# Last column group of the first batch: filter rows in a slot of their own, loads and results on other queues

## The chip, the cores and the metric

One core of a Trainium2 chip runs the whole program. The metric is the device time of one execution in microseconds (us), lower is better. Five engines work side by side: PE (TensorE, matrix products), ACT (ScalarE), DVE (VectorE), POOL (GpSimd) and SP (SyncE, which here only issues transfers). Each takes its instructions strictly in the order in which they were written. A transfer (DMA) is issued by SP, ACT or POOL, moves in the background, and signals when it has landed.

## The reference

```
X = rfft(x, axis=1)                 # x: 8 batches x 3008 x 256
y = irfft(X * (filt_r + 1j*filt_i)) # a filter for each frequency and column
h = y.reshape(24064, 256) @ w_in    # 256 x 2048
out = (h - tanh(h)) @ w_out         # 2048 x 256
```

The weights come as 64-bit floats and are taken apart into 32-bit values on the chip.

## The kernel before, in words

The transform of 3008 points is split as 64 x 47: a product over 64 points, a turn through DRAM, a product over 47 (folded to 24), the filter, and the same way back. All of batch 0 is transformed first, in a prologue of some 79 us, because nothing else can start without it; then the main loop (from L1341) goes over units of the two large products, with the transforms of the later batches laid between them by hand. The order of every engine's instructions is the order of the code (`tc.manual_schedule()`, L1006): nothing is moved by a scheduler, so a waiting instruction holds up all that stands behind it on its engine.

In the prologue the 32 column positions are handled in seven groups: g0 to g5 have five positions (120 rows of a tile), the last one, g6, has two (48 rows). Since 48 rows would fill less than half of the partitions, g6 folds its 256 columns: the second 128 columns go to rows 48 to 95 (`extent`, L154; `KL` = 48, `KH` = 96). For each group:

- `across` (L1057) transposes the first product into a tile `a2` of rows; for g6 it then calls `under` (L1076), which copies the second half of the columns to the lower rows by a transfer on SP.
- `forth` (L403) multiplies by the 24 x 24 matrices; DVE makes sums and differences (L421, L422).
- `filters_of` (L1079) loads the filter rows of the group into one of three slots `filt[g % 3]`: on POOL for g0 and g1, on SP from g2. So g6 takes the slot of g3 and can be loaded only after g3 has been filtered. For g6 there are, besides, a small memset on POOL (L1083), rows that were put into reverse order through the DRAM tensor `filt_d` (L1084), eight loads (L1087; the 23 rows of the mirrored frequencies in two loads of 16 and 7), and an `under` for the filters (L1234, run as L1077).
- `filtered` (L425) does the complex product on DVE, with one addition on POOL for g1 to g4 (L442).
- `back0` (L1098), and `back` (L457) for g6, multiply back; ACT copies the result, and a transfer takes it to DRAM (`ct2`): on POOL for g0 to g4, on ACT for g5, and for g6 half on ACT, half on SP (L469).
- `rest` (L1090) reads `ct2` back in the order that the next product needs: four loads for g0 to g4 on POOL, four for g5 and g6 on SP. The first product that needs them is L582, the beginning of the main part.

The loop at L1225 interleaves the groups: in round g it makes `across(g+2)`, loads the filters of g+2, runs `forth` of g+1, filters g, and multiplies g-1 back. In round 2 it also loads the first 8 rows of batch 1, `x1` (`load_x`, L257, three transfers on SP). Between them DVE turns raw weights into 32-bit values (`converted`, L170, called through `weights`, L241); raw weights are loaded on POOL's queue.

After the loop, `first1` (L1187) makes the first product of `x1`: four steps, stored by two transfers of ACT and two of SP; `warmer` keeps PE at work until `ct2` has come back. In the main loop, `filters_d` (L1291) copies the filters into `filt_d` on POOL, two steps at a time (L1411).

Of the kernel before, what the change touches and what calls it, by code (L numbers as in the profile page):

```python
# [32 lines left out]
KL = SLOTS[-1][1] * NH  # L33
KH = 2 * KL
PAD = 32
# [18 lines left out]
def _consts():  # L54
# [35 lines left out]
    for k, (a, b) in enumerate(((cos, cos), (cos, -sin), (sin, cos), (-sin, -sin),  # L90
                                (cos, twice * cos), (cos, -2 * sin),
                                (sin, twice * cos), (-sin, -2 * sin))):
        for row in (0, KL):
# [23 lines left out]
def kernel(  # L117
# [27 lines left out]
    def dram(t, off, dims):  # L145
        return bass.AP(tensor=t, offset=off, ap=[list(d) for d in dims])
# [7 lines left out]
    def extent(g):  # L154

        n = SLOTS[g][1] * NH
        return (n, DM) if g < len(SLOTS) - 1 else (2 * n, DM // 2)

# [202 lines left out]
    def parts(t, b, g, first_block=0, n=4, step=1):  # L361

        a, s = SLOTS[g]
        rows, w = s * NH, extent(g)[1]
        for h in range(DM // w):
            yield (slice(rows * h, rows * (h + 1)), w,
                   dram(t[b], (first_block * NA + a) * NH * DM + w * h,
                        [[DM, rows], [step * NA * NH * DM, n], [1, w]]))
# [637 lines left out]
    with tc.tile_pool(name="tr", bufs=2) as tr, tc.manual_schedule():  # L1006
# [16 lines left out]
        with tc.tile_pool(name="pro", bufs=1) as pro, \  # L1023
                tc.tile_pool(name="ps0", bufs=6, space=bass.MemoryType.PSUM) as ps0:

            def z0(name, shape):
                return ps0.tile(shape, F32, tag="z", bufs=6, name=name)

# [28 lines left out]
            def across(g):  # L1057

                a, s = SLOTS[g]
                n = s * NH  # L1060
                t = buffer("a2")
                for v in (1, 0):
                    pq = z0("pq", [128, 2, DM])
                    for k in range(2):
                        at = (2 * v + k) * NA + a
                        for h in range(2):
                            nc.tensor.transpose(
                                pq[0:n, k, h * 128:h * 128 + 128],
                                turnt[:, h, at:at + s].rearrange("p a r -> p (a r)"), one)
                    copy = ACT.copy if g or v else V.tensor_copy  # L1070
                    copy(t[0:n, 2 * v:2 * v + 2], pq[0:n])
                if g == len(SLOTS) - 1:
                    under(t)
                return t

            def under(t):  # L1076
                nc.sync.dma_start(t[KL:KH, :, 0:DM // 2], t[0:KL, :, DM // 2:DM])  # L1077

            def filters_of(g):  # L1079

                t, queue = filt[g % 3], G if g < 2 else nc.sync
                if g == len(SLOTS) - 1:
                    G.memset(t[0:1, 2:4], 0.0)  # L1083
                    queue.dma_start(t[NH:KL, 2:4], dram(filt_d, (turned * 8 + 5) * DM,  # L1084
                                                        [[8 * DM, NH], [2 * DM, 2], [1, DM]]))
                for v, row, n, src in filter_rows(g):
                    queue.dma_start(t[row:row + n, v], src)  # L1087
                return t
# [9 lines left out]
            def back0(g, nn):  # L1098

                way = ways(g, 1, KM)  # L1100
                for v in range(2):
                    pe = z0("pe", [128, 2, DM])[0:KM]
                    for k in range(2):
# [5 lines left out]
                    ACT.copy(e1, pe)  # L1109
                    (G if g < len(SLOTS) - 2 else ACT).dma_start(  # L1110
                        next(parts(ct2, 0, g, v, 2, 2))[2], e1)

            pairs = []

# [60 lines left out]
            next(turning)  # L1175

            early = weights(tiles0, jobs[:5], G, began, 5)
# [9 lines left out]
            def first1(x1):  # L1187

                for r in range(0, 8, 2):
                    pf = z0("pf", [128, 2, DM])  # L1190
                    for k in range(2):
                        nc.tensor.matmul(pf[:, k], f0[:, r + k], x1[:, r + k],
                                         start=True, stop=True)
# [5 lines left out]
                    (ACT if r < 4 else nc.sync).dma_start(  # L1199
                        dram(ct1[1], r * DM, [[NH * DM, 128], [1, 2 * DM]]), a1)  # L1200
# [3 lines left out]
            convert(5)  # L1204
            last_g = len(SLOTS) - 1
            summed = (last_g,)
# [18 lines left out]
            for g in range(last_g + 1):  # L1225
                if g == 2:
                    x1 = load_x(big([128, 8, DM], F32, "x1"), 1, 0, 8)
                if g + 2 <= last_g:
                    a2[g + 2] = across(g + 2)
                    fts[g + 2] = filters_of(g + 2)  # L1230
                if g == 3:
                    e2s[0] = load_e2(0, 0, ())
                if g == last_g - 1:
                    under(fts[last_g])  # L1234
                if g < last_g:
                    there[g + 1] = there0(g + 1)
                if g == last_g - 1:
                    way_back()
                next(there[g][0])
# [23 lines left out]
            convert(100)  # L1263
            late = weights(tiles1, jobs[5:], G, ahead, 3,
                           after={6: (0,), 8: (1,), 10: (2, 4)})
            next(late)
            for _ in first1(x1):
                pass
            warmer(8)

        with tc.tile_pool(name="dn", bufs=2) as dn, \
# [69 lines left out]
            for U in range(total + 2):  # L1341
# [45 lines left out]
                def t(k):  # L1387
# [80 lines left out]
```

## Time and profile before

| what | us |
|---|---|
| median of 3 runs | 2559.25 (2557.61 to 2559.39) |
| the profiled execution, its own time | 2556.2 |
| span of its trace | 2554.4 |
| PE busy in the span | 2535.7 |
| first product of the main part (L582) with all its data | 79.00 |

The profiled execution took 1.8 us more than its span, which lies before the first and behind the last instruction, and stands 3.05 us under the median. In the rows below, times are microseconds from the start of the span. A row of a timeline gives start, duration, engine, line, operation, output and input, and in brackets the idle time of the engine before it and what ended it; a row of the chain of waits gives start, duration, and the work. SPq, ACTq and POOLq are the issuing of transfers by these engines; the time to the landing of a transfer stands only in the chain.

### The profile page before, as it was taken

Reading aid. Unit: us, or ns where it says so; the run is one execution under the profiler, and the core shown is the slowest. Engines: PE = TensorE matmul, PEld = TensorE weight load, DVE = VectorE, ACT = ScalarE, POOL = GpSimd, SP = SyncE. Lnnn points to the kernel's source line nnn. Section 1 sums busy time; section 2 is a strip of 40 time slices with the busy share of each in tenths; the row PEclk is TensorE's granted clock in tenths of the full one; section 3 lists DMA queues with packets and bytes.
Section 4 is the critical chain, followed back from the end, with each engine's and each line's share of the span. In section 5 each row is a group of like instructions: output and inputs, shape, how many; then the busy total and the mean of one; then the engine's idle time right before and its main releaser. Section 6 shows DMA issues by size and latency. Waiting matters only on the chain.

```text
span 2554.4 us, 44623 instructions
## 1 busy us (share of the span) xinstructions
PE 2535.7 (99%) x17072; PEld 2173.1 (85%) x17072; DVE 1875.8 (73%) x2262; ACT 1667.1 (65%) x2498; POOL 1484.3 (58%) x1129
## 2 busy tenths in 40 slices
PE   9999999999999999999999999999999999999998
PEld 8678889888898888988888888888889888898887
DVE  6887776887678876888668886688866777555555
ACT  4666666666666666666666666666666666666665
POOL 5356665666466665666555665566645666555552
PEclk9999999999999999999999999999999999999999
DMA  8963224322343323342233322443123322110110
GB/s 233 287 163 103 65 53 109 102 65 61 83 102 91 81 64 94 80 111 59 72 95 99 85 63 61 108 100 97 36 67 85 94 66 52 26 32 18 25 22 19
DMA packets 333828, 212.43 MB, mean 83 GB/s; under 512 B 231841, under 2 KB 304959, under 8 KB 329957
## 3 DMA queue, kind: packets, MB, share of 16 engines
q1 hardware_dynamic: 318471, 184.18, 29.3%
q0 software_dynamic: 11616, 17.44, 2.5%
q10 hardware_dynamic: 3518, 7.87, 0.9%
q8 instruction: 136, 2.23, 0.4%
q14 instruction: 87, 0.71, 0.1%
HBM read 128.75 MB, written 83.39 MB: 83 GB/s over the span
## 4 chain that ended last, share of the span: by engine, by line
PE 94%; DMA 3%; DVE 1%; ACT 1%; issue 0%; SPq 0%; POOL 0%; ACTq 0%; POOLq 0%; DVEq 0%
PE o L795 44%; PE x L623 25%; PE z L623 12%; PE y L623 6%; PE pm L401 3%; PE pu L582 2%; DMA x<-in_x_dram 1%; PE pm L340 1%; DMA filt<-in_filt_r_dram 1%; DMA ct<-a 0%; PE o L857 0%; PE pf L297 0%; DMA filt<-filt 0%; DMA ct<-e 0%; DVE wd L231 0%
## 5 line engine op out<-in xcount | busy, mean ns | idle before, releaser
L795 PE MATMUL o<-t,wd 128*128 128x256 f32 (+1 forms) x3008 | 763.4, 376 | 0.0
L603 POOL TENSOR_TENSOR t<-h 128x512 f32<-128x512 f32 (+1 forms) x186 | 305.4, 1642 | 712.7 <-DVE h L745 704.3
L745 DVE TENSOR_TENSOR h<-h,y 128x1024 f32<-128x1024 f32 (+1 forms) x384 | 580.2, 1511 | 160.1 <-ACT y L741 156.6
L795 PEld LDWEIGHTS o<-t,wd 128*128 128x128 f32 x3008 | 568.8, 190 | 85.8 <-POOL o L827 15.1
L623 PE MATMUL x<-tu,wu 128*128 128x256 f32 (+1 forms) x2256 | 576.1, 378 | 0.0
L795 PE MATMUL o<-h,wd 128*128 128x256 f32 (+1 forms) x2256 | 573.4, 377 | 0.2 <-DVE h L745 0.2
L795 PEld LDWEIGHTS o<-h,wd 128*128 128x128 f32 x2256 | 425.6, 190 | 71.3 <-issue 18.4
L629 ACT COPY s<-x 128x512 f32<-128x512 f32 (+1 forms) x188 | 108.6, 578 | 565.0 <-PE x L623 564.5
L623 PEld LDWEIGHTS x<-tu,wu 128*128 128x128 f32 x2256 | 423.3, 190 | 56.9 <-issue 3.9
L738 ACT ACTIVATE y<-y 128x1024 f32<-128x1024 f32 (+1 forms) x384 | 399.4, 1040 | 12.1
L741 ACT ACTIVATE y<-y 128x1024 f32<-128x1024 f32 (+1 forms) x384 | 399.9, 1041 | 4.6
L735 ACT ACTIVATE y<-h 128x1024 f32<-128x1024 f32 (+1 forms) x384 | 400.4, 1043 | 2.5 <-DVE h L671 1.7
L604 POOL TENSOR_TENSOR t<-h,t 128x512 f32<-128x512 f32 (+1 forms) x186 | 313.9, 1688 | 14.6
L606 POOL TENSOR_TENSOR t<-h,t 128x512 f32<-128x512 f32 (+1 forms) x186 | 303.8, 1633 | 0.0
L605 POOL TENSOR_TENSOR t<-h 128x512 f32<-128x512 f32 (+1 forms) x186 | 289.8, 1558 | 0.0
L629 ACT COPY u<-x 128x512 f32<-128x512 f32 (+1 forms) x376 | 213.3, 567 | 57.0 <-PE x L623 54.1
L671 DVE COPY h<-x 128x512 f32<-128x512 f32 (+1 forms) x188 | 127.8, 680 | 127.2 <-PE x L623 127.1
L623 PE MATMUL y<-ut,wu 128*128 128x256 f32 (+1 forms) x752 | 190.2, 375 | 0.7 <-ACT a L299 0.7
L623 PE MATMUL z<-tu,wu 128*128 128x256 f32 (+1 forms) x752 | 190.2, 375 | 0.4 <-DVE h L679 0.4
L623 PE MATMUL z<-ut,wu 128*128 128x256 f32 (+1 forms) x752 | 190.2, 375 | 0.4 <-DVE h L663 0.4
L623 PE MATMUL x<-ut,wu 128*128 128x256 f32 (+1 forms) x752 | 190.1, 375 | 0.0
L663 DVE TENSOR_TENSOR h<-z,u 128x512 f32<-128x512 f32 (+1 forms) x188 | 127.3, 677 | 72.0 <-ACT u L629 71.1
(208 smaller groups left out, 2809.1 us busy)
## 6 DMA issues: line engine op xcount, KB each, us to landing
ft<-filt SPq DMA_DIRECT2D x28, 1024.0 KB
ct<-nn SPq DMA_DIRECT2D x56, 512.0 KB
e<-ct SPq DMA_DIRECT2D x47, 512.0 KB
a<-ct SPq DMA_DIRECT2D x112, 192.0 KB
out_dram<-ot SPq DMA_DIRECT2D x1248, 16.0 KB
x_sb<-in_x_dram SPq DMA_DIRECT2D x110, 128.0 KB
ct<-a SPq DMA_DIRECT2D x60, 128.0 KB
ct<-x_sb SPq DMA_DIRECT2D x60, 128.0 KB
```

The source lines that it names most:

```text
L603: by.tensor_sub(t[0], b[0][1], b[0][0])
L604: by.tensor_sub(t[1], b[1][1], t[0])
L605: by.tensor_sub(t[2], b[1][1], b[0][1])
L606: by.tensor_sub(t[3], b[1][0], t[1])
L623: nc.tensor.matmul(bank[:, k], wu[:, q - 1, (2 * u + k) * 128:(2 * u + k + 1) * 128], rhs[q - 1], start=(first and k == 0), stop=True, ski ...
L629: ACT.copy(t, X)
L671: V.tensor_copy(h[:, 2, :, 0:w], X)
L735: ACT.activation(y[k], ht[k], AF.Arctan, scale=TURN)
L738: ACT.activation(y[k], y[k], AF.Tanh, scale=BEND)
L741: ACT.activation(y[k], y[k], AF.Square, scale=SCALE, accum_out=y_sums[:, 2 * U + k // 2:2 * U + k // 2 + 1])
L745: V.tensor_mul(ht[k], ht[k], y[k])
L795: nc.tensor.matmul(product(q), wd[:, q - 1, (2 * u + k) * 128: (2 * u + k + 1) * 128], rhs[q - 1][:, k], start=(u == 0 and k == 0 and q == ...
```

## The change

- g6 has its second half at partition 64 instead of 48 (`HB`; `KH` becomes 112). `across` brings it there by the transposes themselves: the one for the second half takes 112 columns, the last 48 of which are the wanted ones, and the one for the first half then overwrites the upper 48 rows. The transfer of `under` for `a2` is gone.
- The filter rows of g6 go to a slot of their own, the buffer of the first raw weights (`raw`, three buffers). `filters_of(last_g)` is called in round 2, ahead of `x1`: a memset of 64 x 1024 elements on POOL, then six loads on SP (the 23 mirrored rows in one load). `under` copies them below in round 3 (two transfers on SP), `turned_in` loads the reversed rows in round 4 (two transfers on SP). Before, all of this came in rounds 4 and 5.
- Results of g3 and g4 are stored on SP instead of POOL. `rest` for g0 to g4 is issued on SP instead of POOL, ahead of the last group's results.
- Raw weights 7 and 8 are loaded in round 5 instead of after the loop (so `weights` starts with four begun), and the first step of weight 3 on ACT is called in round 5.
- `first1` stores all four steps on SP, and its first two steps use half of the buffer `xy` instead of `e1`.
- The prologue has 8 PSUM buffers instead of 6. In the main loop the copies of `filters_d` begin one unit later.

```diff
-KH = 2 * KL
+HB = 64
+KH = HB + KL
@@ weights
-                if (after or k > 1) and n == 2 and k + 1 < len(jobs):
+                if (after or k > 2) and n == 2 and k + 1 < len(jobs):
@@ filter_rows, last group
-                for m, n in ((1, 16), (17, 7)):
-                    yield 2 + v, m, n, dram(src, (NQ * m - a - 1) * DM, [[NQ * DM, n], [1, DM]])
+                yield 2 + v, 1, NH - 1, dram(src, (NQ - a - 1) * DM, [[NQ * DM, NH - 1], [1, DM]])
@@ across
-                        for h in range(2):
+                        for h in (0, 1) if w == DM else (1, 0):
+                            lead, col = (0, h * 128) if w == DM else (HB * h, 0)
                             nc.tensor.transpose(
-                                pq[0:n, k, h * 128:h * 128 + 128],
-                                turnt[:, h, at:at + s].rearrange("p a r -> p (a r)"), one)
+                                pq[0:lead + rows, k, col:col + 128],
+                                turnt[:, h].rearrange("p a r -> p (a r)")[:, NH * at - lead:NH * at + rows], one)
-                if g == len(SLOTS) - 1:
-                    under(t)
+            def turned_in(t):
+                for h in range(2):
+                    nc.sync.dma_start(t[HB * h + NH:HB * h + KL, 2:4, 0:DM // 2],
+                                      dram(filt_d, (turned * 8 + 5) * DM + DM // 2 * h,
+                                           [[8 * DM, NH], [2 * DM, 2], [1, DM // 2]]))
             def under(t):
-                nc.sync.dma_start(t[KL:KH, :, 0:DM // 2], t[0:KL, :, DM // 2:DM])
+                for row, end, n in ((0, NH, 4), (NH, KL, 2)):
+                    nc.sync.dma_start(t[HB + row:HB + end, 0:n, 0:DM // 2],
+                                      t[row:end, 0:n, DM // 2:DM])
@@ filters_of
-                if g == len(SLOTS) - 1:
-                    G.memset(t[0:1, 2:4], 0.0)
-                    queue.dma_start(t[NH:KL, 2:4], dram(filt_d, ...))
+                if g == last_g:
+                    t = pro.tile([128, 512], I64, tag="raw", bufs=3, name="filt_end")
+                    t = t.bitcast(F32).rearrange("p (v n) -> p v n", v=4)
+                    G.memset(t[0:HB], 0.0)
@@ back0
-                    (G if g < len(SLOTS) - 2 else ACT).dma_start(
+                    (G if g < 3 else nc.sync if g < last_g - 1 else ACT).dma_start(
@@ first1
-                    if r == 4:
-                        two = tr.tile([128, 2, 2, DM], F32, tag="a1", bufs=1, name="a1")
-                    a1 = (pro.tile([128, 2, DM], F32, tag="e1", bufs=4, name="a1") if r < 4 else
-                          two[:, r // 2 - 2])
+                    if r % 4 == 0:
+                        two = (tr.tile([128, 2, 2, DM], F32, tag="a1", bufs=1, name="a1") if r else
+                               buffer("xy").rearrange("p (m n) c -> p m n c", m=2))
+                    a1 = two[:, r // 2 % 2]
                     ACT.copy(a1, pf)
-                    (ACT if r < 4 else nc.sync).dma_start(
+                    nc.sync.dma_start(
@@ the loop over the groups
                 if g == 2:
+                    fts[last_g] = filters_of(last_g)
                     x1 = load_x(big([128, 8, DM], F32, "x1"), 1, 0, 8)
                 if g + 2 <= last_g:
                     a2[g + 2] = across(g + 2)
-                    fts[g + 2] = filters_of(g + 2)
+                    if g + 2 < last_g:
+                        fts[g + 2] = filters_of(g + 2)
+                    else:
+                        turned_in(fts[last_g])
                 if g == 3:
+                    under(fts[last_g])
                     e2s[0] = load_e2(0, 0, ())
-                if g == last_g - 1:
-                    under(fts[last_g])
                 if g == last_g - 1:
+                    ahead += [begun(tiles1, job, queue=G) for job in jobs[7:9]]
+                    next(began[3])
                     way_back()
@@ behind it
-            rest(0, SG * (last_g - 1), [G])
+            rest(0, SG * (last_g - 1), [nc.sync])
@@ main loop
-                    if k and U > 1:
+                    if k and U > 2:
                         next(copies, None)
                         next(copies, None)
```

More of the change, by code (lines that the diff above doesn't have):

```diff
@@ L92, in _consts @@
                                 (sin, twice * cos), (-sin, -2 * sin))):
-        for row in (0, KL):
+        for row in (0, HB):
             at = 6 * KM + k * KH + row
@@ L156, in extent @@
         n = SLOTS[g][1] * NH
-        return (n, DM) if g < len(SLOTS) - 1 else (2 * n, DM // 2)
+        return (n, DM) if g < len(SLOTS) - 1 else (KH, DM // 2)
     def ways(g, back, n):
@@ L365, in parts @@
         for h in range(DM // w):
-            yield (slice(rows * h, rows * (h + 1)), w,
+            yield (slice(HB * h, HB * h + rows), w,
                    dram(t[b], (first_block * NA + a) * NH * DM + w * h,
@@ L1023 @@
         with tc.tile_pool(name="pro", bufs=1) as pro, \
-                tc.tile_pool(name="ps0", bufs=6, space=bass.MemoryType.PSUM) as ps0:
+                tc.tile_pool(name="ps0", bufs=8, space=bass.MemoryType.PSUM) as ps0:
             def z0(name, shape):
-                return ps0.tile(shape, F32, tag="z", bufs=6, name=name)
+                return ps0.tile(shape, F32, tag="z", bufs=8, name=name)
             psums.append(z0)
@@ L1059, in across @@
                 a, s = SLOTS[g]
-                n = s * NH
+                rows, w = s * NH, extent(g)[1]
                 t = buffer("a2")
@@ L1065, in across @@
                         at = (2 * v + k) * NA + a
-                        for h in range(2):
+                        for h in (0, 1) if w == DM else (1, 0):
+                            lead, col = (0, h * 128) if w == DM else (HB * h, 0)
                             nc.tensor.transpose(
-                                pq[0:n, k, h * 128:h * 128 + 128],
-                                turnt[:, h, at:at + s].rearrange("p a r -> p (a r)"), one)
+                                pq[0:lead + rows, k, col:col + 128],
+                                turnt[:, h].rearrange("p a r -> p (a r)")[:, NH * at - lead:NH * at + rows], one)
                     copy = ACT.copy if g or v else V.tensor_copy
-                    copy(t[0:n, 2 * v:2 * v + 2], pq[0:n])
-                if g == len(SLOTS) - 1:
-                    under(t)
-                return t
+                    n = extent(g)[0]
+                    copy(t[0:n, 2 * v:2 * v + 2, 0:w], pq[0:n, :, 0:w])
+                return t
+            def turned_in(t):
[3 more added lines that the diff above has]
+                                           [[8 * DM, NH], [2 * DM, 2], [1, DM // 2]]))
             def under(t):
-                nc.sync.dma_start(t[KL:KH, :, 0:DM // 2], t[0:KL, :, DM // 2:DM])
+                for row, end, n in ((0, NH, 4), (NH, KL, 2)):
+                    nc.sync.dma_start(t[HB + row:HB + end, 0:n, 0:DM // 2],
+                                      t[row:end, 0:n, DM // 2:DM])
             def filters_of(g):
                 t, queue = filt[g % 3], G if g < 2 else nc.sync
-                if g == len(SLOTS) - 1:
-                    G.memset(t[0:1, 2:4], 0.0)
-                    queue.dma_start(t[NH:KL, 2:4], dram(filt_d, (turned * 8 + 5) * DM,
-                                                        [[8 * DM, NH], [2 * DM, 2], [1, DM]]))
+                if g == last_g:
+                    t = pro.tile([128, 512], I64, tag="raw", bufs=3, name="filt_end")
+                    t = t.bitcast(F32).rearrange("p (v n) -> p v n", v=4)
+                    G.memset(t[0:HB], 0.0)
                 for v, row, n, src in filter_rows(g):
@@ L1109, in back0 @@
                     ACT.copy(e1, pe)
-                    (G if g < len(SLOTS) - 2 else ACT).dma_start(
+                    (G if g < 3 else nc.sync if g < last_g - 1 else ACT).dma_start(
                         next(parts(ct2, 0, g, v, 2, 2))[2], e1)
+            last_g = len(SLOTS) - 1
             pairs = []
@@ L1204 @@
             convert(5)
-            last_g = len(SLOTS) - 1
             summed = (last_g,)
@@ L1263 @@
             convert(100)
-            late = weights(tiles1, jobs[5:], G, ahead, 3,
+            for _ in first1(x1):
+                pass
+            late = weights(tiles1, jobs[5:], G, ahead, 4,
                            after={6: (0,), 8: (1,), 10: (2, 4)})
             next(late)
-            for _ in first1(x1):
-                pass
             warmer(8)
```

## The prediction

> **What bounds the kernel now.** First the page, then the chain of waits over the first 420 us, then the timelines of the engines named in it. The page:
>
> ```profile
> span 2554.4 us, 44623 instructions
> PE 2535.7 (99%) x17072; PEld 2173.1 (85%) x17072; DVE 1875.8 (73%) x2262; ACT 1667.1 (65%) x2498; POOL 1484.3 (58%) x1129
> ```
>
> PE stands idle for 2554.4 - 2535.7 = 18.7 us in all. The products themselves are untouched, so a gain can only come out of these and out of the fillers in the prologue; a loss has no such limit. The edits lie ahead of the main part's first product (L582, at 79.00), so the question is how far that product moves. The end of the prologue in the chain of waits (start, duration, work):
>
> ```profile
> 37.11 9.92 DMA x<-in_x_dram
> ...
> 57.91 4.07 DMA filt<-in_filt_i_dram
> 62.26 3.03 DMA filt<-filt
> 68.45 0.93 PE pe L464 x4
> 69.80 5.35 DMA ct<-e
> 76.31 2.45 DMA e<-ct
> 79.00 1.15 PE pu L582 x60
> ```
>
> Read from below: the first main product waits for `ct2` to come back, this for the stores of g6's results, these for g6's back products at 68.45, and these for g6's filter rows: the last load landed at 57.91 + 4.07 = 61.98, the copy to the lower rows at 65.29. How long each engine waited there (DVE, then PE):
>
> ```profile
> 55.43 2.15 DVE L433 TENSOR_TENSOR nn<-xy,filt 120x1024 f32<-120x1024 f32 x1 [0.40 <-ACT xy L418]
> 57.62 0.69 DVE L438 TENSOR_TENSOR xy<-xy,filt 120x512 f32<-120x512 f32 x1
> ...
> 60.73 0.42 DVE L422 TENSOR_TENSOR xy<-pb,xy 96x256 f32<-96x256 f32 x1
> 65.47 0.69 DVE L433 TENSOR_TENSOR nn<-xy,filt 96x512 f32<-96x512 f32 x1 [4.32 <-DMA filt<-filt]
> ```
> ```profile
> 65.42 0.59 PE L1106 MATMUL pe<-nn,mats_sb 120*120 120x256 f32 x2
> 68.45 1.76 PE L464 MATMUL pe<-xy,mats_sb 96*96 96x128 f32 x8 [2.44 <-DVE xy L444]
> 70.01 4.66 PE L1192 MATMUL pf<-x,f 128*128 128x256 f32 x16
> 74.51 3.62 PE L1055 MATMUL warm<-f 128*128 128x256 f32 x16
> ```
>
> Two slacks are to be seen. DVE waits 4.32 us for g6's filters; PE waits 2.44, since behind g5's products (done at 65.42 + 0.59 = 66.0) nothing else is ready. So the change's target is real, but it is worth 2.4 us at most at this place, and DVE can lose 4.3 us before g6 comes later than now. In the second row, L438 of g5 at 57.62, the imaginary part of g5's filters is needed: that is the time to remember.
>
> **The change part by part. 1: the loads on SP.** This part decides. SP's issues and POOL's:
>
> ```profile
> 33.02 2.77 SPq L1087 DMA_DIRECT2D filt<-in_filt_i_dram  x3
> 35.88 0.54 SPq L259 DMA_DIRECT2D x<-in_x_dram  x1
> ...
> 37.11 0.64 SPq L265 DMA_DIRECT2D x<-in_x_dram  x1
> 41.06 2.43 SPq L1087 DMA_DIRECT2D filt<-in_filt_r_dram  x3
> ...
> 48.62 2.32 SPq L1087 DMA_DIRECT2D filt<-in_filt_i_dram  x3
> ...
> 55.55 2.62 SPq L1087 DMA_DIRECT2D filt<-in_filt_i_dram  x4
> ```
> ```profile
> 42.66 1.53 POOL L1110 DMA_DIRECT2D ct<-e  x2
> 45.84 1.27 POOL L442 TENSOR_TENSOR nn<-nn,xy 120x512 f32<-120x512 f32 x1 [1.65 <-DVE xy L440]
> ...
> 99.34 0.55 POOL L1293 MEMSET zero<- 128x512 f32 x1
> ```
>
> SP is done with g3's filters at 33.02 + 2.77 = 35.8. Now it goes on with `x1` at once, then g4's filters (from 41.06) and g5's (the last three end at 50.94). After the change the next thing in its order is g6's loads, which write over the memset. The memset stands on POOL at the top of round 2, behind the stores of g0, which end at 42.66 + 1.53 = 44.2. A memset of 512 elements a partition took 0.55 us; 1024 I estimate at 1.0, so it ends at 45.2, just ahead of L442 at 45.84, which it doesn't delay. SP stands from 35.8 to 45.2 and everything behind moves with it. The six loads, at 2.62 / 4 = 0.65 us each, take 3.9: 49.1. `x1` takes as long as now (35.88 to 37.75, 1.9): 51.0. So g4's filters are issued from 51.0 instead of 41.06, 9.9 us later, and g5's by as much: its last load, now issued at about 50.1, at 60.0.
>
> When do they land? At best in 4.07 us, as the load at 57.91 did: 64.1, which is 6.5 us after the 57.62 at which DVE wants it. At worst in 9.92, as `x1`, which again stands just ahead of them: 69.9, 12.3 us late. From both the slack of 4.32 goes off: g6's products come 2.2 to 8.0 us later than now. I take +5.0, the middle: the loads come from a queue with `x1`, g4's and g5's filters all inside 9 us, beside POOL's stores, in a stretch whose engines are full already:
>
> ```profile
> 40.00:60.00 20.00, 19.15 (x99) 16.18 (x100) 19.09 (x25) 8.64 (x16) 14.73 (x18) 1.00 0.94 250
> ```
>
> (The last numbers are PE's clock, the busy share of the transfer engines and GB/s; DVE is busy 19.09 of 20, so it can't catch up either.) g6's own rows, issued by 49.1, with two copies and two reversed rows behind g5's filters, are issued by about 63.4 (four more at 0.65) and land by 67.5 at best, just ahead of DVE's need for them, which is 61.2 now and 61.2 + 6.5 = 67.7 then: what the change set out to hide is hidden, and g4's and g5's filters are late in its place.
>
> **2: results and `rest` on SP.** POOL's and the first results' rows:
>
> ```profile
> 63.53 0.74 POOL L1110 DMA_DIRECT2D ct<-e  x1 [0.98 <-ACT e L1109]
> 65.39 0.55 POOL L1094 DMA_DIRECT2D e<-ct  x1 [1.12 <-issue]
> 67.08 1.51 POOL L1094 DMA_DIRECT2D e<-ct  x3 [1.14 <-issue]
> 68.58 0.75 POOL L174 DMA_DIRECT2D a<-in_moe_w_out_dram  x1
> 69.32 0.75 POOL L174 DMA_DIRECT2D a<-in_moe_w_in_dram  x1
> ```
>
> Now `rest` for g0 to g4 waits on POOL for g4's store (63.53), while SP is free for its half of g6's results at 69.80. After the change these four reads stand on SP in front of that half. g4's store moves with g4's filters, by about 6 us (g5's best case is 6.5), to 69.5; it lands 3.0 to 5.4 us later (the rows 62.26 and 69.80 of the chain), and four reads take about 2 us (65.39 to 68.59 with waits): SP is free at 74.5 to 77, where g6's results are ready at 69.8 + 5.0 = 74.8. Cost 0 to 2.5; with raw weights 7 and 8 now in the same stretch I take +2.5.
>
> **3: raw weights 7 and 8.** Now their two loads start at 68.58 and 69.32, and g6's stores right behind take 5.35 instead of the 3.03 of a small copy at a quiet time. After the change they stand behind POOL's work on g4, which is late itself. The gain is 0 to 2.3; I take -1.0, since the delay of g4 eats most of the head start.
>
> **4: `first1`'s stores.** Its first half goes into `xy`, which ACT's second L180 below must overwrite, so ACT must wait until SP's store has been read.
>
> ```profile
> 80.71 1.25 ACT L180 ACTIVATE xy<-ft 128x512 f32<-128x512 f32 x2
> 83.86 0.53 ACT L696 COPY h<-x 128x448 f32<-128x448 f32 x1 [1.90 <-PE x L693]
> ```
> ```profile
> 80.24 1.02 SPq L1199 DMA_DIRECT2D ct<-a  x2
> ```
> ```profile
> 89.90 1.67 PE L693 MATMUL x<-ut,wu 128*128 128x448 f32 x4
> ```
>
> Issued at 80.24 and landing 5.35 later (the row at 69.80), the store frees `xy` at 85.6; the second L180 then ends 4.4 us later than now, and behind it in ACT's order stands the copy of L696, done at 87.0. PE needs the bank which that copy empties only at 89.90. So nothing waits on PE; DVE's second conversion comes some 2 us later. Between nothing and 2 us, I take +0.5.
>
> **5: the rest.** The 112-column transposes replace 48-column ones; what streams is the unit matrix, 128 columns in both, so PE's time is the same (row below: 8 instructions, 1.04). ACT's copies behind them get half as wide. The copy `a<-a` on SP that goes was never waited for by PE. Eight PSUM buffers instead of six: no idle time of PE in the prologue is put down to a full buffer. Weight 3's first step on ACT falls into a pause of ACT. All cost 0, the cover being that ACT is busy 8.64 of 20 us there. The later copies of `filters_d` leave the transfer engines to the others for one unit; PE's wait in the second row, for ACT's copy of a first product, could gain at most its 0.74: I take -0.2.
>
> ```profile
> 50.28 1.04 PE L1067 MATMUL pq<-one_sb,wd 128*48 128x128 f32 x8
> ```
> ```profile
> 131.65 1.13 PE L623 MATMUL y<-ut,wu 128*128 128x256 f32 x4 [0.74 <-ACT a L299]
> ```
>
> **Sum:** 5.0 + 2.5 - 1.0 + 0.5 - 0.2 = **+6.8 us** on the first main product; behind it PE is full (2535.7 of 2554.4) and hands the delay to the end. The ends of the terms: 2.2 + 0 - 2.3 + 0 - 0.7 = -0.8, and 8.0 + 2.5 + 0 + 2.0 + 0 = +12.5. PE's own order doesn't stretch this: behind g6's products come two blocks of 16 at 3.62, ended at 73.5 + 0.9 + 7.2 = 81.6, before 79.0 + 6.8 = 85.8.
>
> **A rule of the Trainium skill against this change.** The Trainium skill, page "DMA: Bandwidth & Descriptors", section "Why a DMA increments its semaphore by 16 and not by 1", states that a transfer issued by SP or ACT is spread over the largest number of engines up to 16 that divides its slowest dimension. By that rule the new load of 23 rows, 23 being prime, would run on one engine, where the old 16 and 7 ran on 16 and 7. No row of before shows such a load. It makes a rival of its own, priced below.
>
> **The rivals.**
>
> *One engine takes the 23 rows.* Two loads of 23 KB, if they went through one of the 16 engines, would take 46 KB / (250 GB/s / 16 = 15.6) = 2.9 us there, and each piece of `x1` and of g4's and g5's filters on that engine would wait behind them. For: the number of rows is the one thing new about these loads, and they stand ahead of all that is urgent. Against: the load at 57.91 is one of 7 rows, no round number either, and landed in 4.07. It decides from the first such load on, since `x1` and both groups' filters follow it in one queue. Time: 6.8 + 2.9 = +9.7.
>
> *The delay is covered.* g5's filters land in 4.07 us (+2.2 instead of +5.0), SP is free in time (0), the weights leave the tail (-2.3): -0.1 with the last two small terms left out, no change. For it speaks that SP's queue was empty from 35.8 to 45.2, so earlier traffic is gone; against it the 0.94 of the window above.
>
> *Faster: the filters come in time.* One mechanism: the loads behind the memset overtake their delay, because landing times of 9.92 were made by the traffic that now moves away, and g4's and g5's land before DVE asks for them. Landing by 57.62 + 4.32 = 61.9 they cost nothing; landing by 59.5, with 2.4 us to spare, they let g6's products follow at 66.0 instead of 68.45 (-2.4); the stores take 3.03 instead of 5.35 (-2.3), and the 0.74 goes: -5.4. Against it: the last load is issued at 60.0 by my reading, so POOL's memset and with it SP would have to be some 4.5 us earlier than the rows of POOL allow.
>
> *It doesn't do what it says*, g6's filters still being last: they are issued ahead of all others, so I give this nothing of its own.
>
> **How the numbers follow.** My forecast, late filters on SP, gets 0.44; its own range is +3 to +9, and 0.32 of it lies above 0.2%, 0.12 within. The single engine gets 0.22, all slower. Covered 0.22, all within. Faster 0.12: 0.09 over 0.2%, 0.03 within. 0.2% is 5.1 us, about what a measurement of this kernel can tell from no change. That makes slower 0.54, same 0.37, faster 0.09. In the profiled execution's own time the forecast is 2556.2 + 6.8 = 2563.0; that execution stands 3.05 under the median of the runs, so against the median it is 2559.25 + 6.8 = 2566.0. The rivals stand at 2569.0, 2559.2 and 2553.9. The range goes from 2557.0, which leaves out most of the faster case, to 2573.5, which takes in the upper end of the terms and part of the 2.9 on top (+14.3); 0.12 below and some 0.05 above are left out.
>
> **What the new profile would show.** Right: SP issues nothing between 35.8 and about 45.2, then L1087 six times; L259 at about 49; DVE idle before L433 or L438 of g4 and of g5, put down to a filter transfer, 6 us and more in sum; no wait of DVE for g6's rows; PE idle before g4's back products (L1106); L582 first complete at about 86. Wrong: if L438 of g5 starts before 62, if SP is never idle for POOL's memset, or if L582 starts by 80. If the main part's PE idle time (behind L582) grows by more than 2 us, part 4 or the later copies were mis-sized.

## The result

| | us, median | runs | ratio to before, 95% interval |
|---|---|---|---|
| before | 2558.97 (2555.81 to 2566.16) | 18 | |
| after | 2564.37 (2560.34 to 2568.03) | 18 | 1.0019 [1.0012, 1.0026] |

The change costs 5.4 us by the medians (0.21%) and 0.19% by the ratio, so it lies at the 0.2% line drawn in the prediction; the interval leaves out 1. A ratio is taken from all the runs, and below it differs from the quotient of the two medians by up to 0.0007. The forecast was 2566.0. The profiled execution of after took 2563.2 us with a span of 2561.4, so in the profiled pair the span grew by 7.0. In after.py line numbers are higher by 1 (L433 is L434) to 12 (L1331 is L1343); in rows of after the loads of filters are L1095, the memset is L1093.

The page of after (PE idle for 2561.4 - 2537.7 = 23.7 us where before has 18.7, and busy 2.0 us longer), then POOL's timeline around the memset, then SP's:

```profile
span 2561.4 us, 44616 instructions
PE 2537.7 (99%) x17072; PEld 2171.8 (85%) x17072; DVE 1874.7 (73%) x2262; ACT 1666.8 (65%) x2498; POOL 1481.3 (58%) x1121
```
```profile
42.91 1.57 POOL L1118 DMA_DIRECT2D ct<-e  x2
44.48 0.97 POOL L1093 MEMSET filt_end<- 64x1024 f32 x1
46.09 1.27 POOL L443 TENSOR_TENSOR nn<-nn,xy 120x512 f32<-120x512 f32 x1 [0.64 <-DVE xy L441]
```
```profile
33.28 2.39 SPq L1095 DMA_DIRECT2D filt<-in_filt_i_dram  x3
45.48 1.03 SPq L1095 DMA_DIRECT2D filt_end<-in_filt_r_dram  x3
46.56 1.00 SPq L1095 DMA_DIRECT2D filt_end<-in_filt_i_dram  x3
47.66 0.54 SPq L260 DMA_DIRECT2D x<-in_x_dram  x1
...
49.62 2.46 SPq L1095 DMA_DIRECT2D filt<-in_filt_r_dram  x3
...
59.23 2.29 SPq L1095 DMA_DIRECT2D filt<-in_filt_i_dram  x3
```

SP is done with g3's filters at 33.28 + 2.39 = 35.7 and issues nothing until 45.48. The view of SP's waits gives the time to the memset, by name (us in total, times, longest):

```profile
SPq L1095 <- POOL filt_end L1093: 9.7, 1, 9.7
```

The memset itself takes 0.97 us. It costs 9.7 on SP because of where it stands: behind POOL's stores of g0, which end at 44.48. Then come g6's six loads, and only behind them `x1` (47.66; before 35.88), g4's filters (49.62; before 41.06) and g5's last ones (59.23; before 48.62). What the late filters do to DVE and PE, in two timelines of after:

```profile
58.97 1.23 DVE L434 TENSOR_TENSOR nn<-xy,filt 120x1024 f32<-120x1024 f32 x1 [6.99 <-DMA filt<-in_filt_r_dram]
61.74 0.69 DVE L439 TENSOR_TENSOR xy<-xy,filt 120x512 f32<-120x512 f32 x1 [1.55 <-DMA filt<-in_filt_i_dram]
...
64.25 2.00 DVE L434 TENSOR_TENSOR nn<-xy,filt 120x1024 f32<-120x1024 f32 x1 [0.49 <-DMA filt<-in_filt_r_dram]
...
69.86 0.69 DVE L434 TENSOR_TENSOR nn<-xy,filt_end 112x512 f32<-112x512 f32 x1
```
```profile
63.31 1.18 PE L1112 MATMUL pe<-nn,mats_sb 120*120 120x256 f32 x2 [3.95 <-DVE nn L440]
65.22 1.21 PE L1114 MATMUL pe<-nn,mats_sb 120*120 120x256 f32 x2 [0.74 <-POOL nn L443]
...
73.76 1.04 PE L465 MATMUL pe<-xy,mats_sb 112*112 112x128 f32 x8
...
83.92 1.61 PE L582 MATMUL pu<-gt,e 64*64 64x64 f32 x64 [2.21 <-DMA e<-ct]
...
87.44 1.77 PE L693 MATMUL x<-ut,wu 128*128 128x448 f32 x4
```

The last DVE row has no bracket: g6's own filters are in time, where DVE stood 4.32 us for them before. In their place DVE stands 6.99 + 1.55 + 0.49 = 9.03 us for g4's and g5's. g6's back products run at 73.76 instead of 68.45: +5.3. They follow g5's without a pause, so it is not g6's rows that PE waits for, it is everything ahead of them. The end of the chain of waits of after:

```profile
72.89 2.83 DMA ct<-e
75.78 5.19 DMA ct<-e
...
81.39 2.39 DMA e<-ct
...
84.38 1.16 PE pu L582 x60
```

The first main product has all its data at 84.38 (before 79.00): +5.4. That this is also the difference of the medians is chance, since the spans of this pair differ by 7.0.

### The profile page after: what moved, and what is told of

Read it like the earlier page. It is cut to its first block, busy times and chain, and to the rows that moved or that the text cites. A ratio compares the mean times of both kernels' runs of the same rounds, so it can differ in the third digit from the quotient of the medians.

```text
span 2561.4 us, 44616 instructions
## 1 busy us (share of the span) xinstructions
PE 2537.7 (99%) x17072; PEld 2171.8 (85%) x17072; DVE 1874.7 (73%) x2262; ACT 1666.8 (65%) x2498; POOL 1481.3 (58%) x1121
## 4 chain that ended last, share of the span: by engine, by line
PE 94%; DVE 2%; DMA 2%; ACT 1%; issue 0%; POOL 0%; SPq 0%; ACTq 0%; POOLq 0%; DVEq 0%
PE o L795 44%; PE x L623 25%; PE z L623 12%; PE y L623 6%; PE pm L402 3%; PE pu L582 2%; PE pm L341 1%; PE pf L1045 0%; PE warm L1055 0%; DVE h L745 0%; DMA ct<-e 0%; DMA filt<-in_filt_i_dram 0%; DMA ct<-a 0%; DMA x<-in_x_dram 0%; DMA mats_sb<-mats 0%
```

## The experiments

Each ratio is to runs of the kernel before on the same chip; 0.0010 is 2.6 us. "Early kernel" stands for the first one.

**The memset early, and the wait by itself.** A stand is the time for which SP issues nothing. The first kernel takes it away and leaves all else of the change; the second adds only a stand to the kernel before.

```diff
@@ after, the loop over the groups
+                if g == 1:
+                    t = pro.tile([128, 512], I64, tag="raw", bufs=3, name="filt_end")
+                    ends.append(t.bitcast(F32).rearrange("p (v n) -> p v n", v=4))
+                    G.memset(ends[0][0:HB], 0.0)
@@ filters_of(last_g): the tile ends[0], no memset
```

> The changed kernel with one thing moved: the memset of the last group's slot stands at the top of round 1, in POOL's pause before 39.75, and the loads stay where they are. Theory (SP's wait for the memset makes g4's and g5's filters late): SP has no pause of 9.7 us, the six loads go at about 36, g4's filters by 44, DVE waits at most 2 us before g4's and g5's products instead of 9.0, and the first main product (L582) is complete at 76 to 80 instead of 84.3; the whole is 4 to 7 us faster than the changed kernel, so within 3 us of the one before. Rival (the loads of 23 rows on one engine, or SP's longer list as such): the wait goes, but g4's filters stay behind six loads and x1, L582 stays at 82 or later, and the whole is still 3 us or more over the one before.

Measured: 2554.81, 0.9985 [0.9976, 0.9994]. Faster than before, and some 9 us faster than after, where 4 to 7 were expected. SP of the early kernel no longer stands (in its rows the loads of filters are L1093):

```profile
35.45 3.12 SPq L1093 DMA_DIRECT2D filt_end<-in_filt_r_dram  x3
...
40.27 0.54 SPq L260 DMA_DIRECT2D x<-in_x_dram  x1
...
42.24 2.45 SPq L1093 DMA_DIRECT2D filt<-in_filt_r_dram  x3
```

and on PE g6's products come at 65.79, 2.66 before those of the kernel before and 7.97 before those of after:

```profile
65.79 1.04 PE L465 MATMUL pe<-xy,mats_sb 112*112 112x128 f32 x8
...
75.81 0.33 PE L582 MATMUL pu<-gt,e 64*64 64x64 f32 x4 [2.07 <-DMA e<-ct]
76.56 1.15 PE L582 MATMUL pu<-gt,e 64*64 64x64 f32 x60 [0.42 <-issue]
```

The 2.44 us in which PE waited for g6's rows are gone; 2.07 come up again at the next thing that is late, the return of `ct2`, yet the first main product still has its data 2.44 earlier (76.56 against 79.00).

```diff
@@ before, the loop over the groups
                 if g == 2:
+                    t = pro.tile([128, 512], I64, tag="raw", bufs=3, name="alone")
+                    t = t.bitcast(F32).rearrange("p (v n) -> p v n", v=4)
+                    G.memset(t[0:64], 0.0)
+                    nc.sync.dma_start(t[0:NH, 0], dram(filt_r.tensor, 0, [[DM, NH], [1, DM]]))
                     x1 = load_x(...)
```

The tile is read by nothing: the output is that of before.

> The kernel before with the suspected wait alone: at the top of round 2 a memset of 64 x 1024 on POOL into a spare buffer of the raw weights, and on SP, ahead of x1, one load of 24 rows into it, which nothing uses. All else as before, so the last group's filters still come last, in the shared slot. Theory: SP stands from 35.8 to 45.4, x1 and the filters of g4 and g5 are issued 9 us later, DVE waits 7 us or more in g4 and g5, the last group's loads come behind them, and the first main product is complete at 84 to 89 instead of 79.0; the time is 4 to 10 us over the one before. Rival (SP makes up for the wait, since its queue is empty when it ends, and the loss in the changed kernel has other causes): L582 complete by 80.5, time within 1.5 us of before.

Measured: 2567.42 where before stood at 2557.6, 1.0034 [1.0021, 1.0046]. SP issues that one load at 45.37, and the same waits of DVE appear in a kernel with none of the rest of the change:

```profile
55.48 1.23 DVE L433 TENSOR_TENSOR nn<-xy,filt 120x1024 f32<-120x1024 f32 x1 [3.60 <-DMA filt<-in_filt_r_dram]
58.86 0.69 DVE L438 TENSOR_TENSOR xy<-xy,filt 120x512 f32<-120x512 f32 x1 [2.15 <-DMA filt<-in_filt_i_dram]
63.94 1.23 DVE L433 TENSOR_TENSOR nn<-xy,filt 120x1024 f32<-120x1024 f32 x1 [3.06 <-DMA filt<-in_filt_r_dram]
71.89 0.69 DVE L433 TENSOR_TENSOR nn<-xy,filt 96x512 f32<-96x512 f32 x1 [3.16 <-DMA filt<-filt]
```

So the stand costs 0.0034 added to before, and 0.0019 + 0.0015 = 0.0034 taken from after: 8.7 us both ways. They agree more closely than the intervals (some 3 us either way) can show, and the two are not quite the same thing: in before g6's rows stand behind the added load, too, with 3.16 us of DVE's waits in the last row, and PE waits 6.51 us for the copy `a<-a`. The rest of the change is then worth -0.0015, -3.8 us (-2.8 by the two medians).

**The 23 rows in two loads again** (the rival of a single engine).

```diff
-                yield 2 + v, 1, NH - 1, dram(src, (NQ - a - 1) * DM, [[NQ * DM, NH - 1], [1, DM]])
+                for m, n in ((1, 16), (17, 7)):
+                    yield 2 + v, m, n, dram(src, (NQ * m - a - 1) * DM, [[NQ * DM, n], [1, DM]])
```

> The changed kernel with the 23 mirrored rows of the last group loaded in two parts of 16 and 7 again. Theory (the wait on SP): nothing changes but two more issues of 0.3 us; L582 complete at 84 to 85.5, time within 1.5 us of the changed kernel. Rival (23 rows go through one engine and hold up what follows there, 2.9 us): x1 and g4's filters land 2 to 3 us earlier, L582 complete at 81 to 82.

Measured: 2567.21, 1.0031 [1.0019, 1.0042]. Had one engine cost 2.9 us, this kernel would stand near 1.0008, which the interval leaves out: the rival falls. That the 23 rows went through one engine is not shown either, only that no such cost is there. By the medians this kernel is 2.8 us slower than after, where at most 1.5 was expected; the intervals overlap, and a reason is not shown.

**g3's and g4's results and `rest` on POOL again** (step 2).

```diff
-                    (G if g < 3 else nc.sync if g < last_g - 1 else ACT).dma_start(
+                    (G if g < last_g - 1 else ACT).dma_start(
-            rest(0, SG * (last_g - 1), [nc.sync])
+            rest(0, SG * (last_g - 1), [G])
```

> The changed kernel with the stores of g3 and g4 and the four reads of ct2 for g0 to g4 back on POOL, as before. Theory: g6's back products stay at 73.8 (PE), since the filters are as late as ever; L582 moves by at most 0.5 us from SP's side. POOL issues raw weights 7 and 8 ahead of g4's stores, so it may cost up to 1 us instead. L582 complete at 83.3 to 85. Rival (SP's list of results and reads ahead of the last results is what costs, 2.5 us in my sum): g6's stores go out 1 to 2.5 us earlier and L582 is complete by 82.5.

Measured: 2564.39, 1.0022 [1.0013, 1.0031], the median of after. No cost of the order on SP shows, though the two intervals leave room for some 3 us either way. The profiled execution fits neither expectation: g6's products come at 76.41 and the first main product has its data at 85.61. From the one to the other it takes 9.20 us, where after has 10.62 (73.76 to 84.38), so the end of the prologue is 1.4 us shorter there. g6's products come 2.65 later, mostly for what lies ahead of this edit: DVE has g4's second filters at 62.95 instead of 61.74, and POOL's addition behind it takes 2.10 instead of 1.25. A cost of some 1.4 us for the order on SP is neither shown nor excluded.

**Steps 4, 5 and 3 undone in the early kernel, one at a time**, where no stand covers them: `first1` with ACT's queue and the `e1` tiles; the copies of `filters_d` from U > 1; raw weights 7 and 8 behind the loop.

```diff
@@ first1 back
-                    if r % 4 == 0: two = (... buffer("xy") ...)
+                    if r == 4: two = tr.tile([128, 2, 2, DM], F32, tag="a1", bufs=1, name="a1")
...
+                    (ACT if r < 4 else nc.sync).dma_start(
@@ copies back
-                    if k and U > 2:
+                    if k and U > 1:
@@ raws back
-                    ahead += [begun(tiles1, job, queue=G) for job in jobs[7:9]]
-            late = weights(tiles1, jobs[5:], G, ahead, 4,
+            late = weights(tiles1, jobs[5:], G, ahead, 3,
```

> The early memset kernel (2554.8 before) with first1's stores taken back to ACT's queue and e1 tiles (the prediction's step 4, priced +0.5 in a range of 0 to 2). Theory: ACT's copy into xy waits 5.4 us for the load ct<-xy, and that wait hides behind the matmuls of round 1 only in part, so undoing it gives -0.3 to -1.5: 2553.5 to 2554.5. Rival, that PE never sees it: within 0.5 of the early kernel, about 2554.8.

> The early memset kernel with the copies of filters_d taken back from U over 2 to U over 1 (part of the prediction's step 5, priced -0.2). Theory: nothing waits for them, 2554.5 to 2555.5. Rival, that the later copies are where the changed kernel gets back what the wait cost (about -2 to -4 beyond the wait's +9.7): 2557 to 2558.5.

> The early memset kernel with the raw weights 7 and 8 taken back from POOL's early issue (the prediction's step 3, priced -1.0 in a range of -2.3 to 0). Prediction: 2555.8. Theory now, since the one wait on PE that it could remove was 0.2 shorter in the trace: within 0.5 of 2554.8. Rival, that it carries the whole gain of the early kernel: 2557 to 2558.

| early kernel with | us | ratio to before (0.9985 with nothing undone) |
|---|---|---|
| `first1` back | 2555.75 | 0.9986 [0.9977, 0.9995] |
| copies back | 2558.65 | 0.9997 [0.9988, 1.0005] |
| raw weights back | 2556.01 | 0.9989 [0.9981, 0.9998] |

Before stood at 2559.4 there. The raw weights were not taken back in time, only in the order of the code: POOL, which no longer has g3's and g4's stores and `rest` to issue, sends off their two loads at 57.22 and 59.16 in this kernel and at 56.34 and 59.60 in the early one. So this run does not test what earlier loads are worth. `first1` is worth nothing that shows, which means that the expectation from ACT's wait was wrong: in after's timeline of ACT

```profile
86.09 0.68 ACT L181 ACTIVATE xy<-ft 128x512 f32<-128x512 f32 x1
92.15 0.67 ACT L181 ACTIVATE xy<-ft 128x512 f32<-128x512 f32 x1 [5.38 <-DMA ct<-xy]
```

ACT does stand 5.38 us for the store out of `xy`, and PE does not notice. Only the copies moved the middle, by +0.0012, so they got three more kernels.

**The copies alone, in both directions, and later still.** The line of `copies back` the other way round in the kernel before; that line in after; and U > 3 in the early kernel.

> The kernel before with one line of the change: the copies of filters_d from U over 2. The prediction's step 5 priced all its parts together at -0.2. If the later copies alone carry what the early kernel is ahead (its run with the copies taken back stood at 0.9997 of before, the one with them at 0.9985), this is -2 to -3, some 2556 to 2557 where before stands at 2559. Rival, that it is the last group's rows in time and the run with the copies back was only a poor draw: within 1 of before. Rival, that the copies help only together with the earlier raw weights: within 1 of before too, told apart by the next run.

> The changed kernel with the copies taken back to U over 1. If they carry 2.8 us, 2567 where the changed kernel stands at 2564.4 and before at 2559, ratio 1.0032. If nothing depends on them, 1.0019 to 1.0022.

> The early memset kernel with the copies one step later still, U over 3. If their bytes beside the weights and x rows of the first steps are what costs, a little more: 0.9975 to 0.9985 of before. If moving them past U over 1 was enough, 0.9985. If the filter rows come late for the first group that uses them, above 0.999, and a new wait of PE or DVE for filters shows after 150 us.

| | us | ratio to before | the copies from U > 2 give |
|---|---|---|---|
| before, copies from U > 2 | 2556.74 | 0.9994 [0.9985, 1.0003] | -0.0006 |
| after, copies from U > 1 | 2566.01 | 1.0026 [1.0017, 1.0035] | -0.0007 (from 1.0019) |
| early, copies from U > 3 | 2558.33 | 0.9997 [0.9988, 1.0006] | |

Before stood at 2558.24. Three pairs (with the 0.0012 above) point the same way, by 0.0008 in the mean, some 2 us; no single pair settles it, since each has intervals that overlap. U > 3 moves the first copy only from 114.20 to 115.93 (it is at 107.15 from U > 1), and did not go on gaining; its 0.9997 lies where late filter rows were to show, but no wait of PE or DVE for filters shows in its trace behind 100 us. The traces name no wait that the copies make. In the early kernel with the copies back, the view of PE's waits has these as its two longest:

```profile
PE pu L582 <- DMA e<-ct: 3.4, 1, 3.4
PE pf L298 <- DMA x_sb<-in_x_dram: 1.5, 1, 1.5
```

The first ends at 77.57 and the second at 101.12, while the first copy is issued at 107.15, so neither can come from the copies. With U > 3 the second is there as well (1.8), in the early kernel not at all. A size of about 2 us is suggested; a place is not shown.

**Where on SP the six loads stand.** The memset stays late in both. In the first the six loads go behind `x1` and g4's filters, in the second behind `x1` only.

```diff
@@ behind g4
                 if g == 2:
-                    fts[last_g] = filters_of(last_g)
                     x1 = load_x(...)
...
                         fts[g + 2] = filters_of(g + 2)
+                        if g == 2:
+                            fts[last_g] = filters_of(last_g)
@@ x1 ahead
                 if g == 2:
-                    fts[last_g] = filters_of(last_g)
                     x1 = load_x(...)
+                    fts[last_g] = filters_of(last_g)
```

> The changed kernel (2564.4) with the memset where it is, but the last group's six loads put behind x1's and g4's filters on SP. Theory: the +9.6 between the changed kernel and the early one is only the stand of SP at its first load of the last slot; behind g4's filters that load finds the memset done, x1 starts at about 36 to 40 again, and the time is that of the early kernel, 2554 to 2556. Rival, that the six loads' own bytes and issues ahead of g5's filters cost: g5's filters come some 4 us later than in the early kernel and the time is 2557 to 2560. Rival, that the memset on POOL itself costs where it stands: about 2564.

Measured: 2557.02 where before stood at 2559.4, 0.9990 [0.9981, 0.9999]. With the memset where it was, the loss is gone: the memset itself was not the cost, standing at it ahead of others was. The median lies 1 us above the 2554 to 2556 expected, at the edge of the first rival's range (before stood 1.8 higher on this chip than on the early kernel's), and the trace has something for that rival:

```profile
60.04 0.69 DVE L439 TENSOR_TENSOR xy<-xy,filt 120x512 f32<-120x512 f32 x1 [2.52 <-DMA filt<-in_filt_i_dram]
```

g5's filters hold DVE up for 2.52 us, g6's products come at 67.60, and the first main product has its data at 77.67, 1.1 later than in the early kernel. So the six loads ahead of g5's filters probably cost about 1 us.

> The changed kernel with x1's four loads put ahead of the last group's six on SP, which still stand behind the memset. Theory: what costs is that g4's and g5's filters start late; they now start some 2 us sooner (x1's 1.96 us of issues lie ahead of the stand) and the ratio is 1.0011 to 1.0019, some 2561 to 2564 where before is at 2559. Rival: the cost is x1's 1 MB landing beside the filters instead of in the stand; then most of it comes back, 0.9995 to 1.0005, and g4's DVE wait falls from 7 us to under 4. With nothing of either, 1.0019 again.

Measured: 2560.29 where before stood at 2558.72, 1.0005 [0.9996, 1.0014]. The middle is the rival's, the interval reaches into both expectations. DVE's waits in it:

```profile
53.08 1.23 DVE L434 TENSOR_TENSOR nn<-xy,filt 120x1024 f32<-120x1024 f32 x1 [1.61 <-DMA filt<-in_filt_r_dram]
57.15 0.69 DVE L439 TENSOR_TENSOR xy<-xy,filt 120x512 f32<-120x512 f32 x1 [2.85 <-DMA filt<-in_filt_i_dram]
63.47 1.23 DVE L434 TENSOR_TENSOR nn<-xy,filt 120x1024 f32<-120x1024 f32 x1 [4.29 <-DMA filt<-in_filt_r_dram]
```

g4's first wait falls from 6.99 to 1.61, as the rival had it, though g4's loads are issued only 1.74 us sooner (47.88 against 49.62). So, as far as one execution shows it, `x1` in front of the filters made a good part of their lateness at g4. But g5's wait grows from 0.49 to 4.29, and the sum is 8.75 against 9.03: this execution (2562.85) was the slowest of its eleven and doesn't show where the others won their 3.6 us. How the 8.7 us divide between late issues and the company of `x1` stays open.

## Why the prediction came out as it did

- **Step 1, loads on SP (+5.0): right in mechanism, and in size partly by luck.** SP stands from 35.7 to 45.48 (forecast 35.8 to 45.2), the memset took 0.97 (1.0 estimated), `x1` went out at 47.66 (49.1), g4's filters at 49.62 (51.0). They are earlier than forecast since the six loads took 2.1 us (45.48 to 47.56) and not 6 x 0.65 = 3.9: the row that gave 0.65 (55.55) has other loads right ahead of it on SP, as has the early kernel's row at 35.45, where three loads took 3.12. g6's products came 5.3 later. But +5.0 was the middle of 2.2 to 8.0, and the step reckoned with g5's last load, where 8.54 of DVE's 9.03 us are waits for g4's (6.99 + 1.55). Nor is all of the 5.3 DVE's. The row behind which g6's first products can start ends at 72.72, 4.4 later than in before (67.89 + 0.42 = 68.31):

```profile
72.30 0.42 DVE L445 TENSOR_TENSOR xy<-nn 112x256 f32<-112x256 f32 x1
```

  The other 0.9 is PE's own, which was still at g5's products, some of them at half the clock (last section); the sum had no such term. The experiments take the 5.3 apart: 8.0 on g6's products for the stand (65.79 against 73.76), less 2.66 for g6's rows being in time.
- **Step 2, results and `rest` on SP (+2.5): wrong for this kernel.** Undoing it gave nothing that shows (1.0022 against 1.0019). The step set g4's reads in front of g6's stores on a busy SP. In after, the four reads are issued from 73.69 and end at 75.17, and g6's half follows at 75.78:

```profile
73.69 1.48 SPq L1102 DMA_DIRECT2D e<-ct  x4
75.78 1.29 SPq L470 DMA_DIRECT2D ct<-e  x2
```

  ACT's copy of g6's first results ends at 75.33, so SP's half goes out 0.45 behind it (0.02 in before). SP was free at 75.2, in the lower part of the 74.5 to 77 that the step gave; it charged the upper end, for raw weights that POOL had already issued from 65.12. With the stand gone the mechanism is there, though: in the early kernel SP's half goes out at 69.51, 1.94 behind the copy, and with the raw weights back at 69.77, 2.31 behind it. In the latter the chain of waits to the first main product runs through the read that was put in front (66.73):

```profile
66.73 2.98 DMA e<-ct
69.77 3.60 DMA ct<-e
73.78 2.15 DMA e<-ct
```

  No run takes step 2 out of the early kernel, so what it costs there is open.
- **Step 3, raw weights (-1.0): nothing that shows.** In after the weights are issued at 65.12 and 65.84 instead of 68.58 and 69.32, and g6's stores, 10 us behind them, still land in 5.19 where 5.35 stood before; so there it was not weights right ahead that made them longer than 3.03. What frees POOL for these loads is step 2, and the run meant to undo step 3 left them where they were, so step 3 by itself is not tested.
- **Step 4, `xy` (+0.5): nothing that shows**, as the step's reason had it (PE needs the bank later); the 0.5 was caution. ACT stood 5.38 us; the step had its conversion 4.4 us later.
- **Step 5, the rest (-0.2): the copies were probably mis-sized**, some -2 by the three pairs, with the reservation above. All else at 0 was not taken apart.
- **The sum** came to +6.8 and measured +5.4. Of this 5.3 is step 1: from g6's products to the first main product it is 10.62 us in after and 10.55 in before, so that steps 2 to 4, +2.0 in the sum, came to 0.1 together. The 9.20 of the kernel with step 2 undone would fit a loss by step 2 and a gain by step 3 of some 1.4 us each that cancel; single executions don't settle that. On the profiled pair +5.4 lies ahead of the main part, and the other 1.6 of its 7.0 behind it, under the 2 us that were to speak for step 4 or the copies. For 0.74 of it PE waits for rows of x, which in before it did not; the rest has no place yet:

```profile
105.42 1.96 PE L298 MATMUL pf<-x_sb,f 128*128 128x256 f32 x8 [0.74 <-DMA x_sb<-in_x_dram]
```

- **The rivals.** The single engine fell (two loads instead of one: 1.0031, no gain). "Covered" fell, since 9.03 us of DVE's waits are there. "Faster" fell for the kernel as changed: as forecast, the rows of POOL did not allow it. Its outcome came in the early kernel, where g6's products follow without a gap, but not by its mechanism: there no loads overtake a delay, SP has none. The price given was -5.4; -3.8 was measured, and on the path to the first main product -2.44, since 2.07 of PE's wait came back there.

## What to carry to other kernels

A load put at the head of a queue brings along the wait of its destination: look up, on the engine that prepares that destination, when the preparation ends, and who is queued behind the load until then. Here 0.97 us of memset, one engine away, cost 8.7 us, and issuing it a round earlier turned a loss of 0.19% into a gain of 0.15%. When two waits stand one behind the other on the same path (PE's for g6, then for the return of `ct2`), removing the first is worth only its distance to the second. Here the second may itself have grown by the change, since a read in front of a store on one queue showed only once the longer wait was gone.

## What the runs showed of the hardware that was not expected

PE's granted clock fell to half for several us after it had waited, and that stretched the products behind the wait: in after they took 1.06 us a pair (66.22 to 68.78) and then 0.59. The windows of after (the window and its length; PE's busy time and count; its clock, 1.00 being full; busy share of the transfer engines; GB/s):

```profile
60.00:62.00 2.00, 0.00 (x0) 1.00 0.87 269
62.00:64.00 2.00, 0.69 (x2) 0.60 0.52 158
64.00:66.00 2.00, 1.26 (x4) 0.50 0.40 119
66.00:68.00 2.00, 2.00 (x7) 0.50 0.80 151
68.00:70.00 2.00, 2.00 (x8) 0.69 0.82 298
70.00:72.00 2.00, 2.00 (x11) 1.00 0.97 374
```

From the wait's length alone it can't be told when this happens. PE waited 2.07 us ahead of L582 in the early kernel and 2.04 in the one with the raw weights back, whose row comes first here. Then come the windows behind the wait, of the early kernel and of the other:

```profile
76.06 0.33 PE L582 MATMUL pu<-gt,e 64*64 64x64 f32 x4 [2.04 <-DMA e<-ct]
```

```profile
78.00:80.00 2.00, 2.00 (x9) 1.00 1.12 246
```
```profile
78.00:80.00 2.00, 2.00 (x26) 0.50 1.12 269
```

So nearly the same idle time is followed by full clock in one profiled execution and by half clock in another. In the windows of after from 64 to 68 PE is busy for 3.26 us at half the clock, which is 1.6 us of products lost, more than several of the steps priced here. Not all of it counted there: g6's products could not have started before 72.72 in any case, so of their 73.76 at most 1.0 us comes from the clock.
